# Two tokens to a one-hot row set, and four tokens' rows streamed per product, in a parallel attention and expert-lookup kernel

## The chip, the cores and the metric

The kernel runs on one core of a Trainium2 chip. The metric is the device time of one execution in microseconds. Engines are named as the profile names them: PE (TensorE, with its weight loads as PEld), DVE (VectorE), ACT (ScalarE), POOL (GpSimd), SP (SyncE).

## The reference

The input `x` has 2048 tokens of 512 elements. It is normalised, and two branches are added to it: attention with 32 heads of 16 elements that share one key and one value head, and a product-key expert layer, which alone matters here.

```python
    q = jnp.einsum("nd,dhc->nhc", xf, w_q)          # 32 heads
    s1 = jnp.einsum("nhd,ed->nhe", q[..., :dk], k1)  # 64 scores per head
    s2 = jnp.einsum("nhd,ed->nhe", q[..., dk:], k2)
    # the two best of each, the two best sums of the four pairs: top_s, top_e
    g = _softmax(top_s, axis=-1)
    act = _gelu(jnp.einsum("nd,nhkd->nhk", xf, u[top_e]))
    out = jnp.einsum("nhk,nhk,nhkd->nd", g, act, v[top_e])
```

Each token so picks 64 (head, choice) slots out of 4096 experts, each with a gate.

## The kernel before, in words

Tokens are tiled by 128; four tiles make a group of 512. For the groups 0 and 1 the kernel gathers the picked rows of `u` and `v` by indirect DMA and sums them on DVE. For the groups 2 and 3 it works densely (`dense`, L656): it forms the whole gate matrix, tokens by 4096 experts, on TensorE, then computes all 4096 activations of each token (`pact`, L733), weights them with the gate matrix and multiplies with all of `v` (`pout`, L861).

The gate matrix is formed from one-hot rows. An expert number is split into a part `a` of 128 values and a part `b` of 32 values (`batch`, L563, computes both as `df1` and `df2`, L634 to L638). The 64 slots of a token lie on partitions. A gate is kept as two halves, the F16 value of the gate times 8192 and the rest (L647 to L649), so that F16 products lose nothing; the two halves lie on partitions 0 to 63 and 64 to 127 of the same token, and both index rows are stored twice for it. `spread` (L755) transposes the three arrays to slots by tokens on TensorE (`ptd`) and copies them to F16 (`tr`).

Then, for each 16 tokens (`TB`), `onehot` (L779) lets DVE compare a table `io` with the indices: `oa` is 128 rows by 128 values of `a` by 16 tokens (L783), `ob` 128 rows by 32 values of `b` by 16 tokens (L785), which is multiplied by the gates (L786). For each token one product, `oa` of the token as weights (128 by 128) and `ob` of the token as moving data (128 by 32), gives its 128 by 32 gate matrix in PSUM (`pg`, L815). Sixteen of these fill one PSUM tile of 512 columns. ACT copies it in two pieces to a staging tile, sorted by `b` (`copies`, L818 to L820), and after every 64 tokens SP stores it to DRAM (L825, L827). A group has 32 rounds of this (`NQ`), and `onehot` runs two rounds ahead.

The order of the work is written out by hand. PE, DVE, ACT, POOL and SP keep the order in which the program issues instructions. The outer loop (`att_steps`, L1138) makes one turn per attention step: scores `sc` (4 products of 64 rows, in pairs on the two row halves), `pv` (16 products) for the step before, scores again, then `fill` (L1315), which takes the next pieces of the expert layer from a generator (`score_thread`). Each piece yields a cost, and `fill` stops when the costs reach the smaller of a line that rises to `FILL` over the steps and the spent cost plus `MOST`. A round of one-hot products yields 2.0 (L848). While they run (`dense_on` is 2) the step's gathered sums are put behind the fill. Copies and similar work are queued in `POST` and come before the next piece or in the middle of the next step. PSUM tiles of tag `x` (`pg`, `ptd`, `pact`, `psc`, `pout`) share three buffers.

Of the kernel before, what the change touches and what calls it, by code (L numbers as in the profile page):

```python
# [11 lines left out]
F32 = mybir.dt.float32  # L12
F16 = mybir.dt.float16
# [10 lines left out]
P = 128  # L24
# [6 lines left out]
GT = 4  # L31
# [10 lines left out]
NWK = 8  # L42
NIDX = 9
GS = 8192.0
FILL = 948.0
SCALE = DH ** -0.5
LIMIT2 = 25000.0
C_IN = 0.7978845608028654
# [1 line left out]
HOLD = 44  # L50
MOST = 4.0
UNIT = 0.235


@with_exitstack
def tile_kernel(ctx, tc, x, wq, wkv, wo, wqT, kT, uv, ub, vb, out):
# [498 lines left out]
    DT, gated_all = [], []  # L555

    def dense_tiles():
        for _ in range(2):
            da = big.tile([P, 2, D], F32, name="da", tag="da", bufs=2)
            for i in range(2):  # L560
                DT.append(da[:, i, :].rearrange("p (t r s) -> p t r s", t=GT, r=2))

    def batch(ph, c, b):  # L563
        m8, i8 = M8.pop((ph, c, b)), I8.pop((ph, c, b))
        sh = [P, BT, 4]
        T = lambda name, dt=F32, s=sh, bufs=1: small.tile(s, dt, name=name, bufs=bufs)
# [24 lines left out]
        fv = fi.rearrange("p t (h s) k -> p t h s k", s=2)  # L591
        i1a, i1b, i2a, i2b = fv[:, :, :, 0, 0], fv[:, :, :, 0, 1], fv[:, :, :, 1, 0], fv[:, :, :, 1, 1]
        e1, e2 = T("e1"), T("e2")
        stt = V.scalar_tensor_tensor
        den = T("den")
        if ph < NSP:
            idx = T("idx", I32, [P, BT, 4, 2], NIDX)
            i1 = fv[:, :, :, 0, :]
            G_.tensor_scalar(i1, i1, float(E), None, op0=OP.mult)
            G_.tensor_add(e1, i1a, i2b)  # L600
            G_.tensor_add(e2, i1b, i2a)
            G_.tensor_add(i1a, i1a, i2a)
# [21 lines left out]
        df1, df2, dgt = DT[:3]  # L624
# [12 lines left out]
        for r in range(2):  # L637
            G_.tensor_add(df1[:, :, r, w], hi, ii[:, 0])  # L638

        def gates():  # L640
            V.tensor_scalar(den, ex, 2.0, 2.0, op0=OP.mult, op1=OP.add)
            gg = T("gd", F32, [P, BT, 8])
            gv = gg.rearrange("p t (h k) -> p t h k", k=2)
            V.reciprocal(gv[:, :, :, 0], den)
            V.tensor_mul(gv[:, :, :, 1], ex, gv[:, :, :, 0])
            gh = T("gh", F16, [P, BT, 8])
            V.tensor_scalar(gh, gg, GS, None, op0=OP.mult)  # L647
            V.tensor_copy(dgt[:, :, 0, w], gh)
            stt(dgt[:, :, 1, w], gg, GS, gh, op0=OP.mult, op1=OP.subtract)  # L649
            if c == NC - 1:  # L650
                gated_all.append(True)

        exp_later(gates)


    def dense(DG, after):  # L656
# [67 lines left out]
        early = []  # L724
        on_act(lambda: early.extend(half_split(b, 0) for b in range(2)))
        yield 0.0
        df1, df2, dgt = DT[:3]

        def activations(b, us, p):
            n = 0  # L730
# [24 lines left out]
        def spread(n):  # L755
            p = xtile("ptd")
            for j in range(GT):
                nc.tensor.transpose(p[:, j * P:(j + 1) * P], DT[n][:, j].rearrange("p r s -> p (r s)"), ident)
            nc.scalar.copy(tr[:, n, :], p)

        io = kt(F16, (P, P, TB))
        nc.sync.dma_start(io, d_io)
        tr = kt(F16, (P, 3, 512))
        hh = late[0].tile([P, 2, 512], F32, name="gy", tag="gy", bufs=3)
        yield from first(0)
        rest_of_first = first(1)
# [3 lines left out]
            yield 0.45  # L770
        while not gated_all:
            yield None
        spread(2)
        yield 0.45
# [4 lines left out]
        def onehot(q):  # L779
            if q < NQ:  # L780
                tb = q * TB
                oa = kt(F16, (P, P, TB))
                nc.vector.tensor_tensor(out=oa, in0=io, in1=bc(0, tb, P), op=OP.is_equal)  # L783
                ob = obs[:, q % 3]
                nc.vector.tensor_tensor(out=ob, in0=io[:, :NB, :], in1=bc(1, tb, NB), op=OP.is_equal)  # L785
                nc.vector.tensor_mul(ob, ob, bc(2, tb, NB))  # L786
                OH[q] = oa, ob

        def first_gates():
# [10 lines left out]
                    ACC[t] = da[:, i, :]  # L800
                    LIVE.add(t)

        obs = kt(F16, (P, 3, NB, TB))
        onehot(0)
        yield from rest_of_first
        onehot(1)
        for q in range(NQ):
            t0, ql = q // 4 * 64, q % 4
            if ql == 0:
                st = [late[0].tile([P, 16, 64], F32, name="gst", tag="wd", bufs=4) for _ in range(2)]  # L810
            onehot(q + 2)
            oa, ob = OH.pop(q)
            p = xtile("pg")
            for i in range(TB):
                nc.tensor.matmul(p[:, i * NB:(i + 1) * NB], oa[:, :, i], ob[:, :, i], start=True, stop=True)  # L815
            pv_ = p.rearrange("p (t b) -> p b t", b=NB)

            def copies(pv_=pv_, st=st, ql=ql, t0=t0):  # L818
                for hb in range(2):
                    nc.scalar.copy(st[hb][:, :, ql * TB:(ql + 1) * TB], pv_[:, 16 * hb:16 * hb + 16, :])  # L820
                if ql == 3:
# [12 lines left out]
            POST.append((copies, lambda: None))  # L834

            if q in (NQ - 16, NQ - 12):
                later_split((NQ - 16, NQ - 12).index(q))
            if q == NQ - 3:
                on_act(lambda: halves.__setitem__(2, half_split(2, 0)))
            if q == NQ - 3:  # L840
                quiet[0] = 3
            if q == NQ - 2:
# [3 lines left out]
            if q == NQ - 1:  # L846
# [521 lines left out]
```

## Time and profile before

| | |
|---|---|
| median of 3 runs | 1927.19 us |
| lowest, highest run | 1919.88, 1936.14 us |
| the profiled execution | 1931.19 us |
| its span, first to last instruction | 1929.5 us |
| mean granted TensorE clock | 0.98 |
| PE busy | 1865.4 us |
| DVE busy | 1633.0 us |
| ACT busy | 1294.3 us |
| one-hot products `pg` (L815), first and last start | 613.0 and 1528.2 us |

Times in views are microseconds from the start of the span. The one-hot stage comes twice, once for each dense group, at about 609 to 717 us and 1418 to 1528 us. In rows of busy time by window, each engine's busy time in the window is followed by its number of instructions, then come the mean granted clock of TensorE in that window (1.00 is full speed), the share of DMA time and the DMA rate. In rows of groups stand the line, the engine, the operation, the tiles, the shape and the count; then busy time, mean nanoseconds of one instruction, and idle time before it with what ended it. Successive instructions overlap, so the distance of two starts is shorter than an instruction. In the chain of waits, a row is start, duration, engine, tile, line and count.

### The profile page before, as it was taken

The numbers are of one execution on the slowest core, as the hardware profiler recorded it, in microseconds if no ns is written. First come the engines' busy times: TensorE is split into PE (matmuls) and PEld (weight loads), VectorE is DVE, ScalarE is ACT, GpSimd is POOL, SyncE is SP. The second block draws the span as 40 slices with busy tenths as digits, with TensorE's granted clock in tenths as the row PEclk, the third lists the DMA queues.
The fourth block names the chain that finished last, engine by engine and source line by source line (L and its number), as shares of the span: only waits on it lengthen the run. The fifth ranks groups of instructions, "written<-read, shape, count | busy, mean of one in ns | idle before, by whom it ended". The sixth has DMA issues, their size and how long they took to land.

```text
span 1929.5 us, 35007 instructions
## 1 busy us (share of the span) xinstructions
PE 1865.4 (97%) x10990; PEld 995.2 (52%) x10990; DVE 1633.0 (85%) x6381; ACT 1294.3 (67%) x1803; POOL 693.5 (36%) x920
## 2 busy tenths in 40 slices
PE   6879999999999999999999999999999999999998
PEld 4544444555555544555555454555555555555553
DVE  6626788889998976999999897899988879999994
ACT  3336666655557887877877555555578877888873
POOL 1202334334453213343444354344522124344430
PEclk9989999999999989999999999999999999999999
DMA  7856878887673668799889977877645778899882
GB/s 269 300 202 229 291 263 294 287 294 277 231 268 121 216 213 260 248 283 292 267 288 308 353 278 241 295 243 264 216 138 194 267 222 291 271 284 284 283 274 83
DMA packets 245724, 491.14 MB, mean 255 GB/s; under 512 B 93972, under 2 KB 106260, under 8 KB 245532
## 3 DMA queue, kind: packets, MB, share of 16 engines
q0 software_dynamic: 73728, 268.47, 41.4%
q1 hardware_dynamic: 170568, 219.56, 34.9%
q8 instruction: 88, 1.44, 0.3%
q10 hardware_dynamic: 1236, 0.82, 0.1%
q14 instruction: 104, 0.85, 0.1%
HBM read 427.41 MB, written 56.07 MB: 251 GB/s over the span
## 4 chain that ended last, share of the span: by engine, by line
PE 84%; DVE 3%; ACT 2%; issue 1%; DMA 1%; another core or an unknown queue 0%; SPq 0%; ACTq 0%; DVEq 0%
PE pv L341 23%; PE psc L531 18%; PE sc L327 17%; PE pact L733 10%; PE pout L861 9%; PE pg L815 2%; PE pwo L434 2%; ACT pt L330 2%; PE pw L487 2%; DVE oh L783 1%; DMA wk<-dw 1%; DVE xa L1023 1%; DMA wqt<-in_wqT_dram 0%; PE pwt L494 0%; PE pwl L409 0%
## 5 line engine op out<-in xcount | busy, mean ns | idle before, releaser
L330 ACT ACTIVATE pt<-sc 128x1024 f32<-128x1024 f32 x1024 | 994.4, 1026 | 459.2 <-PE sc L327 405.9
L976 POOL DMA_INDIRECT g<-in_uv_dram,idx x512 | 555.0, 1084 | 1009.5 <-DVE xa L1023 531.9
L341 PE MATMUL pv<-pt,vaug 128*32 128x512 f32 x4096 | 508.9, 615 | 0.0
L531 PE MATMUL psc<-wk,xt 128*128 128x512 f32 x1536 | 390.9, 402 | 6.6 <-DVE wk L497 3.5
L327 PE MATMUL sc<-qa,kaug 64*128 64x512 f32 x2048 | 387.0, 453 | 7.7 <-ACT pt L330 6.9
L1023 DVE SCALAR_TENSOR_TENSOR xa<-g,w,xa 128x512 f32<-128x512 f32 x512 | 371.5, 744 | 0.1
L988 DVE CUSTOM_DVE_ANT_0 g<-g,xa 128x512 f32<-128x512 f32 x512 | 335.2, 680 | 6.6 <-DMA g<-in_uv_dram,idx 6.6
L531 PEld LDWEIGHTS psc<-wk,xt 128*128 128x128 f32 x1536 | 279.4, 189 | 110.5 <-issue 40.3
L327 PEld LDWEIGHTS sc<-qa,kaug 64*128 64x128 f32 x2048 | 157.1, 187 | 326.1 <-ACT pt L330 194.3
L341 PEld LDWEIGHTS pv<-pt,vaug 128*32 128x32 f32 x4096 | 108.8, 111 | 255.7 <-issue 254.1
L546 DVE FIND_INDEX8 i<-m,psc 128x8 uint32<-128x64 f32 x1024 | 206.2, 220 | 0.0
L733 PE MATMUL pact<-xt,wk 128*128 128x512 f32 x768 | 196.0, 400 | 0.0
L861 PE MATMUL pout<-wk,wd 128*128 128x512 f32 x768 | 194.9, 402 | 0.2 <-DVE wd L919 0.2
L544 DVE MAX8 m<-psc 128x8 f32<-128x64 f32 x1024 | 146.1, 213 | 41.2 <-PE psc L531 40.0
L861 PEld LDWEIGHTS pout<-wk,wd 128*128 128x128 f32 x768 | 140.8, 188 | 47.4 <-issue 5.5
L733 PEld LDWEIGHTS pact<-xt,wk 128*128 128x128 f32 x768 | 139.4, 188 | 48.6 <-issue 17.9
L864 DVE TENSOR_TENSOR da<-da,pout 128x512 f32<-128x512 f32 x128 | 82.7, 678 | 10.1 <-PE pout L861 8.6
L698 DVE TENSOR_TENSOR wk<-rw,wk 128x512 fp32r<-128x512 f32 x128 | 84.7, 682 | 7.1 <-ACT wk L697 7.1
L783 DVE TENSOR_TENSOR oh<-oh 128x2048 f16<-128x2048 f16 x64 | 78.0, 1219 | 2.3 <-PE pg L815 1.7
L815 PEld LDWEIGHTS <-oh 128*128 128x128 f16 x1024 | 68.4, 163 | 13.6 <-issue 4.8
L815 PE MATMUL pg<-oh 128*128 128x32 f16 x1024 | 73.7, 246 | 0.8 <-DVE oh L786 0.7
L697 ACT CAST wk<-rw 128x512 fp32r<-128x512 f32 x128 | 74.0, 632 | 0.0
(159 smaller groups left out, 1356.4 us busy)
## 6 DMA issues: line engine op xcount, KB each, us to landing
wk<-dw SPq DMA_DIRECT2D x96, 512.0 KB
wqt<-in_wqT_dram SPq DMA_DIRECT2D x32, 512.0 KB
dw<-wk SPq DMA_DIRECT2D x32, 512.0 KB
rw<-in_ub_dram SPq DMA_DIRECT2D x64, 256.0 KB
rw<-in_vb_dram SPq DMA_DIRECT2D x64, 256.0 KB
gy<-dg SPq DMA_DIRECT2D x64, 256.0 KB
qa<-dqh SPq DMA_DIRECT2D x128, 64.0 KB
g<-in_uv_dram,idx POOLq DMA_INDIRECT x512
```

Of the source, the lines that this page charges most:

```text
L327: nc.tensor.matmul(p[:, b, :], kaug[o:o + 64, kc * P:(kc + 1) * P], QA[u][o:o + 64, i, :], start=True, stop=True)
L330: nc.scalar.activation(pt, p, AF.Exp, scale=SCALE)
L341: nc.tensor.matmul(PV[u][32 * j:32 * j + 32, :], vaug[:, kc, :], pt[:, b, :], start=kc == 0, stop=kc == 15)
L531: nc.tensor.matmul(p, XT[k][:, a, j * P:(j + 1) * P], WC[n_][k][:, bb, :], start=n == 0, stop=n == 11)
L544: nc.vector.max(m8[:, jb, s, :], p[:, s * E:(s + 1) * E])
L546: nc.vector.max_index(i8[:, jb, s, :], m8[:, jb, s, :], p[:, s * E:(s + 1) * E])
L733: nc.tensor.matmul(p, us[:, a, k * P:(k + 1) * P], XT[k][:, c, :], start=n == 0, stop=n == 11)
L815: nc.tensor.matmul(p[:, i * NB:(i + 1) * NB], oa[:, :, i], ob[:, :, i], start=True, stop=True)
L861: nc.tensor.matmul(p, wd[0][:, a, j * P:(j + 1) * P], vs[:, c, :], start=n == 0, stop=n == 5)
L976: nc.gpsimd.indirect_dma_start(out=gt, out_offset=None, in_=uv, in_offset=bass.IndirectOffsetOnAxis(ap=IDX[ph, c, ti][:, s:s + 1], axis=0))
L988: nc.vector.tensor_tensor_reduce(u, u, XN[TPH * ph + ti], scale=1.0, scalar=0.0, op0=OP.mult, op1=OP.add, accum_out=a[:, i:i + 1])
L1023: nc.vector.scalar_tensor_tensor(acc, v, w[:, i:i + 1], acc, op0=OP.mult, op1=OP.add)
```

## The change

The rows of a product are shared by two tokens instead of two gate halves: partitions 0 to 63 hold the 64 slots of an even token, partitions 64 to 127 those of the odd token after it. A round covers 16 pairs, 32 tokens, so there are 16 rounds. `oa` and `ob` are compared once per pair; `ob` is then multiplied by the upper and by the lower gate halves into two tiles. The index arrays are stored once, the gate halves as arrays of their own, four arrays in all, and `spread` brings the parity apart with an identity matrix read in steps of two.

For each pair there are four products instead of two: for each gate half `r` one on each row half `h`, with 64 rows. Those of the two gate halves add up in PSUM, and each row half has a PSUM tile of its own. The moving data are `WIDE` = 4 tokens' `ob` rows, 128 columns, though only the first 32 belong to the weights' token; the other 96 are overwritten by the products of the following tokens. `copies` writes every second token. The round's cost, the constants and the points at which later work is queued are fitted to 16 rounds.

```diff
-FILL = 948.0
+FILL = 935.0
+WIDE = 4
...
     def dense_tiles():
-        for _ in range(2):
-            da = big.tile([P, 2, D], F32, name="da", tag="da", bufs=2)
-            for i in range(2):
-                DT.append(da[:, i, :].rearrange("p (t r s) -> p t r s", t=GT, r=2))
+        da = big.tile([P, 4, GT, 64], F32, name="da", tag="da", bufs=2)
+        DT.extend(da[:, i] for i in range(4))
...
-        for r in range(2):
-            G_.tensor_add(df2[:, :, r, w], hi, ii[:, 1])
+        G_.tensor_add(df2[:, :, w], hi, ii[:, 1])
...
-            V.tensor_copy(dgt[:, :, 0, w], gh)
-            stt(dgt[:, :, 1, w], gg, GS, gh, op0=OP.mult, op1=OP.subtract)
+            V.tensor_copy(dgh[:, :, w], gh)
+            stt(dgl[:, :, w], gg, GS, gh, op0=OP.mult, op1=OP.subtract)
...
-        NQ = 512 // TB
+        NQ = 512 // (2 * TB)
...
             for j in range(GT):
-                nc.tensor.transpose(p[:, j * P:(j + 1) * P], DT[n][:, j].rearrange("p r s -> p (r s)"), ident)
-            nc.scalar.copy(tr[:, n, :], p)
+                for h in range(2):
+                    nc.tensor.matmul(p[64 * h:64 * h + 64, 64 * j:64 * j + 64], DT[n][:, j, :], ident[:, h::2],
+                                     start=True, stop=True)
+            nc.scalar.copy(tr[:, n, :], p[:, :256])
...
-                ob = obs[:, q % 3]
-                nc.vector.tensor_tensor(out=ob, in0=io[:, :NB, :], in1=bc(1, tb, NB), op=OP.is_equal)
-                nc.vector.tensor_mul(ob, ob, bc(2, tb, NB))
+                ob = obs[:, q % 2]
+                nc.vector.tensor_tensor(out=ob[:, 1], in0=io[:, :NB, :], in1=bc(1, tb, NB), op=OP.is_equal)
+                for i in range(2):
+                    nc.vector.tensor_mul(ob[:, i], ob[:, 1], bc(2 + i, tb, NB))
...
-            onehot(q + 2)
+            onehot(q + 1)
             oa, ob = OH.pop(q)
-            p = xtile("pg")
+            ps_ = [xtile("pg") for _ in range(2)]
             for i in range(TB):
-                nc.tensor.matmul(p[:, i * NB:(i + 1) * NB], oa[:, :, i], ob[:, :, i], start=True, stop=True)
+                for r in range(2):
+                    for h in range(2):
+                        o = slice(64 * h, 64 * h + 64)
+                        n = min(WIDE, TB - i)
+                        nc.tensor.matmul(ps_[h][:, i * NB:(i + n) * NB], oa[o, :, i],
+                                         ob[o, r, :, i:i + n].rearrange("p b t -> p t b"),
+                                         start=r == 0, stop=r == 1)
...
-            yield 2.0
+            yield 3.6
```

More of the change, by code (lines that the diff above doesn't have):

```diff
@@ L623, in batch @@
             dense_tiles()
-        df1, df2, dgt = DT[:3]
+        df1, df2, dgh, dgl = DT
         ii = T("ii", F32, [P, 2, BT, 8])
@@ L633, in batch @@
         G_.tensor_scalar(hi, ii[:, 1], 32.0, -32.0, op0=OP.is_ge, op1=OP.mult)
-        for r in range(2):
-            G_.tensor_add(df2[:, :, r, w], hi, ii[:, 1])
+        G_.tensor_add(df2[:, :, w], hi, ii[:, 1])
         G_.tensor_scalar(hi, hi, -2.0, None, op0=OP.mult)
-        for r in range(2):
-            G_.tensor_add(df1[:, :, r, w], hi, ii[:, 0])
+        G_.tensor_add(df1[:, :, w], hi, ii[:, 0])
         def gates():
@@ L726, in dense @@
         yield 0.0
-        df1, df2, dgt = DT[:3]
         def activations(b, us, p):
@@ L757, in spread @@
             for j in range(GT):
-                nc.tensor.transpose(p[:, j * P:(j + 1) * P], DT[n][:, j].rearrange("p r s -> p (r s)"), ident)
-            nc.scalar.copy(tr[:, n, :], p)
+                for h in range(2):
+                    nc.tensor.matmul(p[64 * h:64 * h + 64, 64 * j:64 * j + 64], DT[n][:, j, :], ident[:, h::2],
+                                     start=True, stop=True)
+            nc.scalar.copy(tr[:, n, :], p[:, :256])
         io = kt(F16, (P, P, TB))
         nc.sync.dma_start(io, d_io)
-        tr = kt(F16, (P, 3, 512))
+        tr = kt(F16, (P, 4, 256))
         hh = late[0].tile([P, 2, 512], F32, name="gy", tag="gy", bufs=3)
@@ L772, in dense @@
             yield None
-        spread(2)
-        yield 0.45
+        for n in (2, 3):
+            spread(n)
+            yield 0.45
         dense_on[0] = 2
@@ L801, in load_totals, with copies @@
                     LIVE.add(t)
-        obs = kt(F16, (P, 3, NB, TB))
+        obs = kt(F16, (P, 2, 2, NB, TB))
         onehot(0)
         yield from rest_of_first
-        onehot(1)
         for q in range(NQ):
-            t0, ql = q // 4 * 64, q % 4
+            t0, ql = q // 2 * 64, q % 2
             if ql == 0:
                 st = [late[0].tile([P, 16, 64], F32, name="gst", tag="wd", bufs=4) for _ in range(2)]
-            onehot(q + 2)
+            onehot(q + 1)
             oa, ob = OH.pop(q)
-            p = xtile("pg")
+            ps_ = [xtile("pg") for _ in range(2)]
             for i in range(TB):
[L815 to L821, printed above, removed]
+                for r in range(2):
[5 more added lines that the diff above has]
+                                         start=r == 0, stop=r == 1)
+            def copies(ps_=ps_, st=st, ql=ql, t0=t0):
+                for h in range(2):
+                    pb = ps_[h].rearrange("p (t b) -> p b t", b=NB)
+                    for hb in range(2):
+                        to = st[hb][:, :, ql * 2 * TB:(ql + 1) * 2 * TB].rearrange("p b (t h) -> p b t h", h=2)
+                        nc.scalar.copy(to[:, :, :, h], pb[:, 16 * hb:16 * hb + 16, :])
+                if ql == 1:
                     def part(b0, b1, st=st, t0=t0):
@@ L834, in dense @@
             POST.append((copies, lambda: None))
-            if q in (NQ - 16, NQ - 12):
-                later_split((NQ - 16, NQ - 12).index(q))
-            if q == NQ - 3:
+            if q in (NQ - 8, NQ - 6):
+                later_split((NQ - 8, NQ - 6).index(q))
+            if q == NQ - 2:
                 on_act(lambda: halves.__setitem__(2, half_split(2, 0)))
-            if q == NQ - 3:
+            if q == NQ - 2:
                 quiet[0] = 3
-            if q == NQ - 2:
+            if q == NQ - 1:
                 dense_on[0] = 3
@@ L845, in dense @@
                 later_split(2)
-            if q == NQ - 1:
                 later_split(3)
-            yield 2.0
+            yield 3.6
         held, ready, used = [], [], [0]
```

## The prediction

> **What bounds the kernel now.** I read the page first, then the one-hot stage in the windows of busy time, then the chain of waits, then single groups.
>
> ```profile
> PE 1865.4 (97%) x10990; PEld 995.2 (52%) x10990; DVE 1633.0 (85%) x6381; ACT 1294.3 (67%) x1803; POOL 693.5 (36%) x920
> PEclk9989999999999989999999999999999999999999
> ```
>
> TensorE is busy 97% of the span, so its work sets the time. The digits of the granted clock hide what matters here; the windows show it. The stage with the one-hot products comes twice; the first two rows are its two passes (17 attention steps each), then two undisturbed steps with 32 products, one with 16, and every step with a lowered clock. A step is one turn of the attention loop: sc, pv, sc, then whatever fills it. The third number is busy PE; PEclk stands third from the end.
>
> ```profile
> core 0: us, PE busy (x) PEld busy (x) DVE busy (x) ACT busy (x) POOL busy (x), PEclk, DMA share, GB/s
> 609.47:710.30 100.83, 99.82 (x905) 52.23 (x904) 94.42 (x193) 85.45 (x142) 21.48 (x18) 0.90 0.63 204
> 1426.52:1528.33 101.81, 97.76 (x907) 52.30 (x905) 94.23 (x189) 86.33 (x143) 23.23 (x20) 0.92 0.63 210
> 615.21:620.56 5.35, 5.35 (x60) 3.10 (x58) 5.21 (x14) 4.92 (x9) 0.00 (x0) 1.00 0.08 21
> 1511.37:1516.72 5.35, 5.35 (x58) 3.10 (x57) 5.28 (x11) 5.00 (x10) 0.00 (x0) 1.00 0.98 317
> 705.59:710.30 4.71, 4.53 (x42) 2.18 (x40) 4.43 (x12) 4.71 (x10) 1.15 (x1) 1.00 0.98 349
> 636.93:642.88 5.95, 5.95 (x42) 2.27 (x40) 5.81 (x17) 3.88 (x8) 0.00 (x0) 0.71 0.98 302
> 654.20:661.29 7.09, 7.09 (x58) 3.51 (x56) 6.99 (x13) 5.60 (x12) 0.12 (x1) 0.76 0.51 199
> 677.45:684.54 7.09, 7.09 (x58) 3.50 (x57) 7.02 (x12) 5.25 (x9) 3.35 (x3) 0.76 0.55 187
> 684.54:691.60 7.06, 7.06 (x60) 3.35 (x58) 6.38 (x14) 5.20 (x10) 1.15 (x1) 0.76 0.84 263
> 691.60:698.63 7.03, 7.03 (x59) 3.34 (x57) 5.28 (x12) 5.08 (x10) 0.00 (x0) 0.76 0.46 171
> 698.63:705.59 6.96, 6.96 (x59) 3.30 (x57) 5.88 (x12) 4.82 (x8) 3.34 (x3) 0.75 0.39 109
> 1431.80:1439.44 7.64, 7.22 (x56) 3.45 (x57) 7.57 (x14) 6.10 (x10) 2.11 (x2) 0.78 0.47 128
> 1439.44:1446.43 6.99, 6.99 (x60) 3.44 (x58) 6.85 (x17) 5.00 (x9) 0.00 (x0) 0.76 0.70 236
> 1457.25:1464.29 7.04, 5.75 (x59) 3.23 (x58) 6.94 (x16) 4.85 (x9) 2.75 (x3) 0.94 0.99 308
> 1464.29:1471.32 7.03, 7.03 (x42) 2.68 (x40) 5.96 (x13) 4.21 (x8) 0.00 (x0) 0.57 0.57 209
> 1494.11:1500.09 5.98, 5.98 (x42) 2.48 (x40) 5.84 (x15) 4.58 (x9) 0.00 (x1) 0.71 0.73 239
> 1528.33:1535.34 7.01, 7.01 (x35) 3.00 (x34) 4.90 (x16) 6.39 (x12) 0.91 (x1) 0.76 0.52 150
> ```
>
> An undisturbed step with 32 products takes 5.35 us and one with 16 takes 4.71. Those with 42 instructions on PE hold 16 products, the others of the stage 32. The eleven rows with a lowered clock exceed their clean length by 1.24 (5.95 against 4.71) to 2.32 us (7.03 against 4.71). The one at 1457.25 is mostly a wait (PE busy 5.75 of 7.04); the other ten exceed by 17.2 us together. The clock explains it: 0.76 over 7.09 us is 3.4 us at half rate, which costs 1.7 us, and 7.09 less 5.35 is 1.74. The chain of waits shows a clean step (first four rows) and a step with the low clock:
>
> ```profile
> 615.28 0.66 PE sc L327 x4
> 615.94 1.85 PE pv L341 x16
> 617.79 0.66 PE sc L327 x4
> 618.46 2.17 PE pg L815 x32
> ...
> 678.18 3.37 PE pv L341 x16
> 681.55 0.79 PE sc L327 x4
> 682.34 2.27 PE pg L815 x32
> ```
>
> It is TensorE all the way round. The low clock falls on pv (3.37 for 1.85) and hardly on the one-hot products (2.27 for 2.17). So the products seem to bring the clock down and the attention pays.
>
> **The change part by part.** First the products. They go from 1024 of 128 rows and 32 columns to 2048 of 64 rows and 128 columns, in row pairs; the instruction order of the changed kernel shows 32 bursts of 64, one burst to a step, where 36 bursts of 16 or 32 stood. So 32 tokens still cost 32 turns of the array, if the two halves run side by side.
>
> ```profile
> L531 PE MATMUL psc<-wk,xt 128*128 128x512 f32 x1536 | 390.9, 402 | 6.6 <-DVE wk L497 3.5
> L327 PEld LDWEIGHTS sc<-qa,kaug 64*128 64x128 f32 x2048 | 157.1, 187 | 326.1 <-ACT pt L330 194.3
> L815 PE MATMUL pg<-oh 128*128 128x32 f16 x1024 | 73.7, 246 | 0.8 <-DVE oh L786 0.7
> 618.39 2.23 PE L815 MATMUL pg<-oh 128*128 128x32 f16 x32
> 617.72 0.30 PEld L327 LDWEIGHTS sc<-qa,kaug 64*128 64x128 f32 x4 [0.84 <-ACT pt L330]
> 25.94 0.44 PE L218 MATMUL pv_t<-ident,kv 32*128 32x32 f32 x4 [0.20 <-ACT kv L203]
> 591.35 3.69 PE L531 MATMUL psc<-wk,xt 128*128 128x512 f32 x15
> 605.76 1.04 PE L758 MATMUL ptd<-ident,da 128*128 128x128 f32 x8
> ```
>
> Today's turn is (2.23 - 0.246) / 31 = 64 ns for 32 columns. A 512-column product turns over in (3.69 - 0.40) / 14 = 235 ns, 0.46 ns per column, so 32 columns are 15 ns of streaming: three quarters of the 64 ns is a floor, not data. 128 columns at 0.46 are 59 ns and fit under it. That the halves run together is what sc does already: its 64-row products come in such pairs, and 4 take 0.66 us, 0.33 per pair of 512 columns, where two in series would be 0.47. Bounds for a pair: 59 ns below (streaming alone), 128 above (two floors in series). Between them lie 83 (a quarter of sc's 0.33) and 107 (the 128-column F32 transpose ptd, (1.04 - 0.29) / 7 with a latency between pg's 0.246 and psc's 0.40). I take 64: the same floor, since the stream fits, and pg is the nearest row. A burst then keeps its length. A pair dearer by 1 ns costs 1.0 us over 1024 pairs.
>
> Second the clock. Streaming fills 15 of 64 ns today and 59 of 64 after it, about as dense as the psc products, and through the stretch of those between the passes the page's clock digits are 9. I take the 17.2 us as gone, and 1.6 us of the step at 1528.33, which has the low clock just behind the stage.
>
> Third the sum for the stage. The two passes take 202.64 us and hold 62 of the 64 groups of 16 tokens; the other two lie in mixed steps, 16 x 64 ns and a switch of 0.2, 2.4 together. They hold 34 attention steps; after it 32 hold all groups, and two go to steps elsewhere at 0.66 + 1.85 + 0.66 = 3.17 each. So like for like it is 202.6 + 2.4 - 6.3 = 198.7 us today. Clean steps would be 28 x 5.35 + 6 x 4.71 = 178.1; 24.5 are excess, 17.2 of it clock and 7.3 other waits, 0.21 per step, which I keep. A burst of today also has an edge: 2.17 us from its first product to the next sc is 31 turns and 0.19, where a turn is 0.064; the array goes over from 128-row to 64-row work there, and the other way at the start. The new products are 64-row work as sc is, so up to 0.12 at each end can go. I count one end, as ScalarE stands near: its busy time in the clean steps is 4.92 and 5.00, and its work per 32 tokens stays. So 32 x (5.35 + 0.21 - 0.12) = 174.1, a gain of 24.6. Bounds of the step: 5.0 below (ScalarE), 5.9 above (rival E).
>
> Fourth the work off the chain.
>
> ```profile
> L783 DVE TENSOR_TENSOR oh<-oh 128x2048 f16<-128x2048 f16 x64 | 78.0, 1219 | 2.3 <-PE pg L815 1.7 <-issue 0.4 <-ACT oh L759 0.2
> L785 DVE TENSOR_TENSOR oh<-oh 128x512 f16<-128x512 f16 x64 | 26.7, 417 | 0.0
> L786 DVE TENSOR_TENSOR oh<-oh 128x512 f16<-128x512 f16 x64 | 27.2, 425 | 2.3
> L820 ACT COPY gst<-pg 128x256 f32<-128x256 f32 x128 | 42.8, 405 | 0.2 <-PE pg L815 0.2
> ```
>
> VectorE makes 32 wide comparisons instead of 64, 32 narrow ones instead of 64, and the same 64 gate products: (1219 + 417) x 32 = 52 us less. I count nothing for it: the chain runs over TensorE, the 94.4 busy us of VectorE in a pass of 100.8 at most gave some of the small waits, which I kept. The copies stay 128 of 256 elements; writing every second word could cost or save a little, and the next step's exponentials cover it. GpSimd loses two additions per batch and is 36% busy. SP's stores of the gates keep their number and size. The spreading of indices takes 64 small products and 8 copies where 24 and 6 stood: 64 x 64 ns less 24 x 107 is 1.5 us, and I count 2. The pacing constants (3.6 per 32 tokens for 4.0, the target lower by 13) move work between steps, not in amount.
>
> Sum: -24.6 - 1.6 + 2.0 = -24.2. The profiled execution took 1931.19 us (span 1929.5), so 1907; the median of the runs shown is 4.0 lower, 1927.19, and gives 1903. I say 1904.
>
> **The rivals.** B, strided reading (ends slower). The 128 columns lie 32 bytes apart, and no row streams such columns for longer than the floor. If each costs 0.86 ns, as a column of sc's weights does ((0.30 - 0.187) us from the first pair's load to the second's, 128 columns), a pair takes 110 ns and adds 1024 x 46 ns = 47 us: 1951. It decides from 64 + 23 = 87 ns per pair on. At the far end, were all of today's 64 ns reading, it would be 256 ns, +197 us, 2101. Against the far end: L218's 32 columns lie side by side and take the same ((0.44 - 0.222) / 3 = 73 ns with the first start). The Trainium skill, SBUF — State Buffer, section Specifications (TRN2), states that each access that crosses to a new 16-byte line pays a penalty, which would make every one of these columns pay; it gives no figure, and no row here shows it.
>
> C, halves in series: 128 ns per pair, +65 us, 1969. sc's pairs speak against it.
>
> D, the clock still falls: then 17.2 + 1.6 us stay, 1923. For it: the chip's rule isn't in the trace, and PE reads busy through all of the stage. The Trainium skill, TensorE: Matmul & The Clock Gate, Part 1, ties the half rate to an idle window of about 3.4 us; by that rule a TensorE that reads busy 99% should not drop, and wider products would mend nothing. The 0.76 steps with PE busy 7.09 of 7.09 disagree with it, unless short streams count as idle.
>
> E, a new wait: a burst now fills two of three PSUM tiles at once, and both are emptied only in the next step, behind two exponentials, where the first tile of a pair was emptied within the burst's own step. With 0.46 us per step for it (about one copy, 0.405), steps take 5.9: +15, 1919.
>
> **How the numbers follow.** Forecast 0.50, B 0.20, C 0.11, D 0.09, E 0.10. The forecast's own range is 1893 (steps of 5.1, by ScalarE's bound) to 1916. The range 1893 to 1952 takes in E, D and most of B, and leaves out C and B's far end. About 1% can be told from no change, 1908 to 1946. Faster: 0.76 of the forecast, 0.38. Same: the rest of it 0.12, E, D, 0.02 of B, 0.33. Slower: B and C, 0.29.
>
> **What would show it.** 2048 products; bursts of 64 in 2.1 to 2.3 us; PEclk 1.00 through both passes and pv at 1.85; steps of 5.3 to 5.6; L783's group at 39 us. Bursts of 3.5 us with a full clock mean B, 4.1 mean C; 0.76 in the windows means D; sc waiting on exponentials, or products on copies, with a clean clock means E.

## The result and the profile after

The changed kernel takes 2135.44 us (median of 4 runs, 2131.53 to 2137.17) beside 1931.66 of the kernel before (4 runs): ratio 1.1065, 95% interval 1.1033 to 1.1097. It is slower by a tenth, where 1904 was forecast. The profiled execution has a span of 2135.4 us, 205.9 more than the 1929.5 of before. The page of the kernel after, its first line, the granted clock, and the groups of the products and of attention:

```profile
PE 2060.9 (97%) x12118; PEld 1096.8 (51%) x12118; DVE 1588.7 (74%) x6317; ACT 1297.3 (61%) x1805; POOL 679.9 (32%) x888
PEclk9989999999997769999999999999977689999999
L818 PE MATMUL pg<-oh 64*128 64x128 f16 (+3 forms) x2048 | 231.2, 397 | 0.6 <-ACT gst L827 0.3
L342 PE MATMUL pv<-pt,vaug 128*32 128x512 f32 x4096 | 538.9, 646 | 0.0
L328 PE MATMUL sc<-qa,kaug 64*128 64x512 f32 x2048 | 402.4, 469 | 10.8 <-ACT pt L331 7.1
```

TensorE is still the bound, 97% busy, with 195.5 us more to do. The one-hot products went from 73.7 to 231.2 us of busy time. The two dips of the clock, to 7 and 6 in tenths, are the two one-hot passes. Attention, which the change doesn't touch, pays for them: pv took 508.9 and takes 538.9, sc took 387.0 and takes 402.4. The windows of the two passes (16 steps each) and of two steps, with the columns of the prediction's first windows:

```profile
616.66:808.99 192.33, 191.85 (x1410) 101.75 (x1410) 71.38 (x160) 83.92 (x139) 21.04 (x18) 0.71 0.33 106
1530.34:1730.68 200.34, 197.66 (x1504) 106.20 (x1505) 75.90 (x173) 89.75 (x149) 22.99 (x21) 0.73 0.32 103
638.76:651.38 12.62, 12.62 (x94) 6.38 (x92) 4.16 (x11) 4.99 (x8) 0.00 (x0) 0.64 0.71 236
651.38:662.87 11.49, 11.49 (x95) 6.31 (x92) 1.89 (x5) 5.03 (x8) 0.00 (x0) 0.80 0.01 1
```

The two steps shown take 12.62 and 11.49 us, and nearly all the others 11.4 to 12.7, where 5.44 was forecast. A clock of 0.71 over 192.33 us is 192.33 x 0.29 / 0.5 = 112 us at half rate, where the first pass of before, 0.90 over 100.83 us, had 20. PE is busy all through (191.85 of 192.33), and DVE and ACT are busy for 71 and 84 us of it, so no other engine holds it up. The chain of waits over a step and a half (start, duration, engine, tile, line, count):

```profile
651.58 1.01 PE sc L328 x4
652.59 2.81 PE pv L342 x16
655.40 0.66 PE sc L328 x4
656.07 7.02 PE pg L818 x59
663.09 1.01 PE sc L328 x4
664.10 3.57 PE pv L342 x16
```

The burst of 64 products takes 7.02 us; a burst for the same 32 tokens took 2.17. Over 32 bursts that is 32 x 4.85 = 155 us. The scores behind a burst take 1.01 for 0.66 and pv 2.81 to 3.57 for 1.85; by the two groups above that is 30.0 + 15.4 = 45.4 us. The two together, 200.6, are nearly all of the 205.9. What one turn costs is seen in a narrow window of the timeline of PE, three pairs of four tokens:

```profile
644.67 0.90 PE L818 MATMUL pg<-oh 64*128 64x128 f16 x6
```

The six products run from the first start to the last end in 0.90 us; less one product of 0.417 (the median of the line) that is two turns of 0.24 us. The medians over all pairs, from the starts in the trace's records, are 240 ns for four tokens, 181 to 184 for three, 122 to 126 for two and 65 for one. So a turn of four tokens costs 1.87 ns per column, and it takes the same 240 ns at full and at half clock. In 28 of the 32 bursts the two halves of a pair start 0 to 42 ns apart, 10 in the median; in the other four one half runs most of a turn ahead of the other. The work off the chain is as it was counted (minimum, median and maximum in ns, then first and last start):

```profile
L782 DVE TENSOR_TENSOR oh<-oh x32: 1214/1220/1227, 614.0 to 1697.7; 128x2048 f16<-128x2048 f16 x32
L784 DVE TENSOR_TENSOR oh<-oh x32: 417/422/427, 615.1 to 1706.5; 128x512 f16<-128x512 f16 x32
L786 DVE TENSOR_TENSOR oh<-oh x64: 424/425/428, 615.6 to 1707.5; 128x512 f16<-128x512 f16 x64
L827 ACT COPY gst<-pg x128: 381/422/456, 629.8 to 1734.2; 128x256 f32<-128x256 f32 x128
```

### The profile page after: what moved, and what is told of

Same layout as the page of the kernel before. It is cut to its first block, busy times and chain, and to the rows that moved or that the text cites. A ratio compares the mean times of both kernels' runs of the same rounds, so it can differ in the third digit from the quotient of the medians.

```text
span 2135.4 us, 37163 instructions
## 1 busy us (share of the span) xinstructions
PE 2060.9 (97%) x12118; PEld 1096.8 (51%) x12118; DVE 1588.7 (74%) x6317; ACT 1297.3 (61%) x1805; POOL 679.9 (32%) x888
## 4 chain that ended last, share of the span: by engine, by line
PE 81%; DMA 4%; DVE 4%; ACT 2%; issue 2%; SPq 0%; another core or an unknown queue 0%; ACTq 0%; DVEq 0%
PE pv L342 22%; PE psc L532 16%; PE sc L328 15%; PE pg L818 11%; PE pact L729 7%; PE pout L867 6%; PE pwo L435 2%; ACT pt L331 2%; DMA gy<-dg 1%; PE pw L488 1%; DVE xa L1029 1%; DMA rw<-in_vb_dram 1%; DMA wk<-dw 1%; DVE g L994 1%; DMA dinv<-rc 0%
## 5 line engine op out<-in xcount | busy, mean ns | idle before, releaser
L342 PE MATMUL pv<-pt,vaug 128*32 128x512 f32 x4096 | 538.9, 646 | 0.0
L328 PE MATMUL sc<-qa,kaug 64*128 64x512 f32 x2048 | 402.4, 469 | 10.8 <-ACT pt L331 7.1
L328 PEld LDWEIGHTS sc<-qa,kaug 64*128 64x128 f32 x2048 | 166.9, 197 | 338.1 <-ACT pt L331 165.4
L818 PE MATMUL pg<-oh 64*128 64x128 f16 (+3 forms) x2048 | 231.2, 397 | 0.6 <-ACT gst L827 0.3
L818 PEld LDWEIGHTS <-oh 64*128 64x128 f16 x2048 | 159.0, 145 | 77.5 <-issue 10.0
L1017 DVE SCALAR_TENSOR_TENSOR w<-gth,ga 128x4 f32<-128x4 f32 x128 | 20.6, 161 | 208.2 <-ACT gth L1010 207.8
```

What stands on the lines that cost most here:

```text
L328: nc.tensor.matmul(p[:, b, :], kaug[o:o + 64, kc * P:(kc + 1) * P], QA[u][o:o + 64, i, :], start=True, stop=True)
L342: nc.tensor.matmul(PV[u][32 * j:32 * j + 32, :], vaug[:, kc, :], pt[:, b, :], start=kc == 0, stop=kc == 15)
L818: nc.tensor.matmul(ps_[h][:, i * NB:(i + n) * NB], oa[o, :, i], ob[o, r, :, i:i + n].rearrange("p b t -> p t b"), start=r == 0, stop=r == 1)
```

## The experiments

The first theory, S, was that the 32-byte step of the columns costs about 1.8 ns each. Its rivals were H, that products on 64-row halves are slow, and C, that the clock is the main cause. After the first four kernels S was narrowed to L: each 16-byte line that the moving rows open costs about 1.9 ns. Beside it K was put for the clock: it is kept up by the columns that stream per nanosecond. Each kernel is compared with the kernel before on the same chip.

**One token to a product (w1).**

```diff
-WIDE = 4
+WIDE = 1
```

> The changed kernel with WIDE = 1: each of the 2048 64-row products streams the 32 columns of its own token only. Theory S (stride): a streamed column that lies 32 bytes from the one before it costs about 1.8 ns of TensorE, whatever the clock, so 128 columns took 240 ns per pair and 32 take about 62; a burst of 64 products then lasts 2.0 to 2.2 us instead of 7.3, and the kernel comes to 1890 to 1935 us. Theory H (halves): the pairs of 64-row F16 products are slow in themselves (two halves, or two sums into PSUM); then a pair stays above 120 ns, a burst above 3.9 us, and the kernel above 1985 us. Theory C (clock): the time went mainly to the half-rate clock; then the burst hardly shortens and the low stretches stay, over 2050 us. By S the low clock stays in part, as 32 columns of 62 ns are as thin as before.

Measured: 1930.21 us (10 runs), ratio 1.0031, interval 1.0011 to 1.0051. The page's group of w1, then its timeline from the scores ahead of a burst to those behind it:

```profile
L818 PE MATMUL pg<-oh 64*128 64x32 f16 x2048 | 75.4, 246 | 2.8 <-ACT gst L827 2.8
645.63 0.73 PE L328 MATMUL sc<-qa,kaug 64*128 64x512 f32 x4
646.21 2.35 PE L818 MATMUL pg<-oh 64*128 64x32 f16 x64
648.32 0.76 PE L328 MATMUL sc<-qa,kaug 64*128 64x512 f32 x4
```

A turn is (2.35 - 0.246) / 31 = 68 ns. The whole loss goes with the three additional tokens, and 0.3% is left, so the pairing and the 64-row halves cost little: H falls. DVE has as much less to do as in the changed kernel, and the time doesn't show it. At the edges of the burst something is won: from scores to burst 0.58 us for 0.66, from burst to scores 2.11 for 2.17. The windows of w1's two passes:

```profile
615.76:703.62 87.86, 85.70 (x1410) 51.25 (x1410) 69.40 (x157) 81.94 (x139) 21.97 (x18) 1.00 0.71 229
1418.78:1523.61 104.83, 99.41 (x1503) 56.56 (x1502) 73.96 (x170) 88.02 (x149) 23.47 (x21) 0.93 0.59 196
```

The clock is 1.00 in the first pass and 0.93 in the second, where the kernel before had 0.90 and 0.92, although w1 streams as few columns per nanosecond as that kernel. A short thin burst, then, lowers the clock at some times and not at others.

**The widening without the pairing (before_wide).** The kernel before, with products of 128 rows that stream four tokens:

```diff
-                nc.tensor.matmul(p[:, i * NB:(i + 1) * NB], oa[:, :, i], ob[:, :, i], start=True, stop=True)
+                n = min(WIDE, TB - i)
+                nc.tensor.matmul(p[:, i * NB:(i + n) * NB], oa[:, :, i],
+                                 ob[:, :, i:i + n].rearrange("p b t -> p t b"), start=True, stop=True)
```

> The kernel before with the widening alone: 1024 products of 128 rows, each streaming the strided columns of four tokens (128) instead of one (32). Theory S: a product turns over in 240 ns instead of 64, 32 of them take 7.5 us instead of 2.1, and with the clock lower for longer the kernel comes to 2110 to 2160 us: the whole loss without any pairing. Theory H: 64 to 70 ns, 1905 to 1935 us.

Measured: 2109.76 us, one run. The group and a burst:

```profile
L817 PE MATMUL pg<-oh 128*128 128x128 f16 (+3 forms) x1024 | 230.2, 401 | 0.1
655.87 7.20 PE L817 MATMUL pg<-oh 128*128 128x128 f16 x32
```

The burst is as long as that of the changed kernel, with 32 products for its 64. The widening alone makes nearly the whole loss.

**The same columns side by side (contig).** The changed kernel with the narrow rows stored token by token, so that the 128 columns of a product are contiguous:

```diff
-        obs = kt(F16, (P, 2, 2, NB, TB))
+        obs = kt(F16, (P, 2, 2, TB, NB))
...
-                                         ob[o, r, :, i:i + n].rearrange("p b t -> p t b"),
+                                         ob[o, r, i:i + n, :].rearrange("p t b -> p (t b)"),
```

> The changed kernel with WIDE = 4, but the narrow one-hot rows stored token by token, so that the 128 streamed columns are one run of 256 bytes; VectorE writes them in steps of 64 bytes for it. Theory S: pairs at 55 to 70 ns, bursts of 1.8 to 2.2 us, clock 1.00 in the stage, 1890 to 1920 us if VectorE's steps cost nothing, up to 1940 if its narrow groups double (3 x 32 x 0.42 us is 40 us). Theory H: pairs at 240 ns, about 2135 us.

Measured: 2071.87 us (4 runs), ratio 1.0755, interval 1.0719 to 1.0791. Its products are cheap and its DVE is not; the groups of the page:

```profile
L819 PE MATMUL pg<-oh 64*128 64x128 f16 (+3 forms) x2048 | 100.8, 271 | 117.7 <-DVE oh L787 113.3
L787 DVE TENSOR_TENSOR oh<-oh 128x512 f16<-128x512 f16 x64 | 154.4, 2413 | 2.5
L785 DVE TENSOR_TENSOR oh<-oh 128x512 f16<-128x512 f16 x32 | 78.0, 2439 | 0.0
```

A turn with 128 contiguous columns takes about 63 ns at full clock (the median of the records), 107 at half clock. So the forecast's sentence that 128 columns fit under the floor holds for contiguous columns. But the writes of DVE now lie 64 bytes apart, and an instruction takes 2.4 us where 0.42 stood; PE waits 113.3 us for it. The kernel shows the price of a turn; its time, far above the 1890 to 1940 that were expected, is DVE's and says nothing on the turn.

**Runs inside a line (runs, runs8).** A run here is a stretch of adjacent values. The layout of the changed kernel, with the columns streamed value by value: the four tokens of a value lie side by side, 8 bytes, then comes the next value. In runs8 the window of tokens also ends at every eighth token, so that no run crosses a 16-byte line; this is the diff of runs8, and runs keeps `min(WIDE, TB - i)`:

```diff
-                        n = min(WIDE, TB - i)
-                        nc.tensor.matmul(ps_[h][:, i * NB:(i + n) * NB], oa[o, :, i],
-                                         ob[o, r, :, i:i + n].rearrange("p b t -> p t b"),
+                        n = min(WIDE, 8 - i % 8)
+                        nc.tensor.matmul(ps_[h].rearrange("p (b t) -> p b t", t=TB)[:, :, i:i + n], oa[o, :, i],
+                                         ob[o, r, :, i:i + n],
```

> The changed kernel with WIDE = 4, but the same 128 columns streamed in the order in which they lie: for each value of b the four tokens side by side (runs of 4 F16 elements, 8 bytes), written to PSUM in that order too. Theory S by place in memory: only a jump of 32 bytes costs, 32 jumps as with one token, so a pair takes 60 to 70 ns, a burst 2.0 to 2.2 us; the array then streams nearly all the time, the granted clock stays at 1.00 in the stage, and the kernel comes to 1890 to 1920 us. Theory S by element (any column not read as one long run costs 1.8 ns): pair 240 ns, about 2135 us. Theory H: the pair stays at 240 ns, about 2135 us.

> The run that streams tokens side by side, with windows that end at a 16-byte border (up to four tokens, fewer for the last three of each eight). In that run the windows that started at tokens 5, 6 and 7 of eight took about 118 ns per pair and the others 62 to 75. Theory L (line): TensorE pays about 1.9 ns for each 16-byte line that it opens, 32 lines without a crossing and 64 with one; then every pair takes 60 to 75 ns, the products take 35 to 38 us per pass instead of 42.8, and the kernel is 10 to 16 us faster than that run, 1908 to 1920 us here, if the clock stays up. Theory S by element: no change from that run, 1931 us. If the fewer columns let the clock fall, 5 to 10 us are lost again.

Measured: runs 1931.37 us (10 runs), ratio 1.0032, interval 1.0007 to 1.0056; runs8 1921.69 (12 runs), ratio 0.9982, interval 0.9966 to 0.9998. First a burst of runs, then one of runs8, then the window of a pass of runs8:

```profile
649.55 2.80 PE L818 MATMUL pg<-oh 64*128 64x128 f16 x64
```

```profile
649.27 2.46 PE L818 MATMUL pg<-oh 64*128 64x128 f16 x64
618.49:707.50 89.01, 87.06 (x1409) 52.99 (x1410) 69.44 (x157) 82.00 (x139) 21.94 (x18) 1.00 0.71 227
L867 PE MATMUL pout<-wk,wd 128*128 128x512 f32 x768 | 197.9, 405 | 9.1 <-DVE gy L910 5.1
```

The same 128 columns from the same tile cost 62 to 82 ns a turn, if they stay in 32 lines. In runs the windows that start at token 5, 6 or 7 of eight reach into a second line for every value, which makes 64 lines, and those turns take 105 to 130 ns. The clock in the pass is 1.00, where before it was 0.90; as w1 had 1.00 in its first pass too, one pass alone proves little. Both kernels took longer than expected (1890 to 1920 for runs, 1908 to 1920 for runs8). The last row shows what takes part of the gain back: pout waits 9.1 us, where the kernel before waited 0.2; in the changed kernel it is 5.1, in w1 4.2.

**The widening alone, inside a line (before_runs8, before_runs3, before_runs2).** The kernel before, 128 rows to a product, with at most four, three or two tokens:

```diff
+WIDE = 4
...
+                n = min(WIDE, 8 - i % 8)
+                nc.tensor.matmul(p.rearrange("p (b t) -> p b t", t=TB)[:, :, i:i + n], oa[:, :, i],
+                                 ob[:, :, i:i + n], start=True, stop=True)
```

> The kernel before with the widening alone, in its harmless form: 128-row products, up to four tokens side by side within a 16-byte line, PSUM in that order. Theory L: a product keeps its 64 to 70 ns. Theory K (clock by streamed columns): up to 128 columns in 66 ns keep the granted clock at 1.00 in the stage, the 17 to 19 us that the low stretches cost come back, and the kernel takes 1900 to 1912 us against 1921. If the clock falls for another reason than thin streams (waits, the switch of the array between row sizes), the low stretches stay and the time is 1915 to 1930. If the pairing itself were what keeps the clock up, the same.

> The same with three tokens (96 columns). Theory K: clock 1.00 in both one-hot stages, products 62 to 72 ns, time 1908 to 1915, beside the 1914 of four tokens. If the time lies above 1917, the gain of four tokens was not the clock's alone.

> The kernel before with products that stream two tokens (32 columns, in two runs of adjacent tokens, so that no run crosses a 16-byte line) instead of four or one. Theory L (each 16-byte line of the moving rows that is opened costs about 1.9 ns): a product keeps the 62 to 76 ns of its neighbours with four and with one. Theory K (the clock is kept by the number of columns that a turn streams): with half the columns of the four-token kernel the clock in the one-hot stages stays at 1.00 if 64 columns are enough, and the time is 1905 to 1914, at or below the 1914 of four tokens since the products are shorter; if 64 are too few, half-clock stretches of several us come back and the time is 1915 to 1922. A rival, that the clock fell in the kernel before by chance of the run and not by the columns, gives 1920 to 1928 with stretches like its 20 us.

Measured: four tokens 1913.82 us (12 runs), ratio 0.9942, interval 0.9925 to 0.9959; three tokens 1911.94 (6 runs), 0.9943, 0.9922 to 0.9963; two tokens 1914.84 (12 runs), 0.996, 0.9942 to 0.9977. All three are faster than both kernels, by a small amount (0.4 to 0.6% against the kernel before) that is clear of the noise; four tokens came out 2 us above the range that was expected. The window of a pass and three groups of the kernel with four tokens, then the window of a pass with two:

```profile
605.39:705.40 100.01, 98.19 (x952) 56.43 (x952) 97.19 (x202) 92.27 (x153) 21.44 (x18) 1.00 0.67 216
L342 PE MATMUL pv<-pt,vaug 128*32 128x512 f32 x4096 | 493.6, 598 | 0.0
L328 PE MATMUL sc<-qa,kaug 64*128 64x512 f32 x2048 | 380.9, 448 | 7.0 <-ACT pt L331 6.8
L817 PE MATMUL pg<-oh 128*128 128x128 f16 (+3 forms) x1024 | 78.9, 243 | 2.8 <-DVE oh L787 2.8
```

```profile
606.70:706.52 99.82, 96.25 (x952) 54.31 (x951) 97.09 (x201) 91.82 (x153) 21.48 (x18) 1.00 0.68 216
```

The clock is 1.00 in the pass with four tokens and with two (64 columns). Over all executions of these kernels the mean clock of the whole span has a median of 0.99, in the kernel before 0.98. Attention, which the edit doesn't touch, gets back 15.3 us in pv and 6.1 in sc against the profiled execution of before, one of its longer ones; the products take 5.2 more. By the medians the gain is 11 us. It comes without the pairing, and where the clock is back, so it is the clock's. Which of the three is best is not told apart: their intervals overlap.

**The line as the unit (g4, g4_wide).** The changed kernel with narrow rows in groups of four tokens, so that the columns of one token lie 8 bytes apart, two to a line. g4 streams one token to a product, g4_wide four, three, two and one, as the groups end. The diff is that of g4_wide; in both, DVE's writes are reordered to match:

```diff
-        obs = kt(F16, (P, 2, 2, NB, TB))
+        obs = kt(F16, (P, 2, 2, TB // 4, NB, 4))
...
-                        n = min(WIDE, TB - i)
+                        n = 4 - i % 4
...
-                                         ob[o, r, :, i:i + n].rearrange("p b t -> p t b"),
+                                         ob[o, r, i // 4, :, i % 4:].rearrange("p b t -> p t b"),
```

> The changed kernel with one token per product (32 columns) and the narrow rows stored in groups of four tokens, so that neighbouring columns lie 8 bytes apart, two to a 16-byte line. Theory L: 16 lines cost 30 ns, so a pair is bounded by what else there is, the weight load; if that is shorter than 62 ns, pairs fall to 40 to 55 ns and the products to 25 to 30 us per pass; if the load is the floor of 60, pairs stay at 60 to 66. VectorE writes runs of 8 bytes now: where writing every 64 bytes made its narrow operations 2400 ns instead of 420, runs of four could take 600 (little change in the time) to 2400 (about 2070 us).

> The changed kernel with its second rows stored in groups of four tokens, so that a product's columns lie 8 bytes apart, two to each 16-byte line, instead of 32 bytes apart; products stream four, three, two and one tokens, as the groups end. Theory L: 128 columns open 64 lines, about 120 ns per pair, 96 columns about 90, 64 and 32 columns about 62; some 85 ns on average, a few half-clock us, 1925 to 1960. If the cost is by the column that isn't adjacent to the last, whatever the step: 240, 180, 120 and 62 ns, and a time between 2040 and 2140. If only steps over some width cost: 62 to 66 ns throughout and 1918 to 1930.

Measured: g4 1928.58 us (10 runs), ratio 1.0024, interval 1.0007 to 1.004; g4_wide 1936.6, one run. A burst of g4, then one of g4_wide and the window of its pass:

```profile
642.28 2.18 PE L819 MATMUL pg<-oh 64*128 64x32 f16 x64
```

```profile
650.64 2.82 PE L820 MATMUL pg<-oh 64*128 64x128 f16 x64
618.38:712.17 93.79, 92.82 (x1409) 58.79 (x1410) 69.86 (x159) 82.55 (x139) 21.97 (x18) 1.00 0.67 216
```

With half the lines to open, one token's turn stays at 63 ns, so this is a floor in which the reading of the moving rows has no part; but a product of g4 is shorter, 210 ns in the median for 246. What sets the floor was not tried. Every product also loads 128 columns of weights, and these lie 32 bytes apart in all of these kernels. In g4_wide the turns are 120, 93, 64 and 50 ns for 64, 48, 32 and 16 lines; the 50, behind three longer turns, is below the floor, so the floor isn't a fixed cost of a product. The two longer ones fit L: 64 x 1.87 = 120, 48 x 1.87 = 90. The reading by the single column (240) and that of a free 8-byte step (63) both fall. All turns side by side, medians at full clock, good to some 3 ns:

| columns and how they lie | lines opened | ns per turn |
|---|---|---|
| 128, 32 bytes apart (the change, before_wide) | 128 | 240 |
| 96, 32 bytes apart | 96 | 181 to 184 |
| 128, 8 bytes apart (g4_wide) | 64 | 120 |
| 64, 32 bytes apart | 64 | 122 to 126 |
| 128, in runs of four (runs8) | 32 | 76 |
| 32, 32 bytes apart (w1) | 32 | 66 |
| 32, 8 bytes apart (g4) | 16 | 63 |
| 128, contiguous (contig) | 16 | 63 |

L doesn't account for the whole row of runs8: 32 x 1.87 is 60, and it takes 76. Its products also write PSUM in runs of four; whether the rest lies there was not tried.

**What brings the clock down (w1_x3, runs8_x3).** w1 and runs8 with every pair of products issued three times over, which makes bursts of 6 to 7 us like those of the change, once thin and once dense:

```diff
-                for r in range(2):
+                for r in (0, 1) * 3:
```

> The changed kernel with one token to a product (32 columns, 32 bytes apart) and every pair of products issued three times over, the same result each time: bursts of about 6.3 us at half a column per nanosecond, as long and as thin as those of the changed kernel, but without a wide product. The two repeats add 2048 turns of 65 ns, 133 us, to the 1930 of one token to a product. Theory K (the clock goes where few columns per nanosecond stream for long): half-clock stretches of some 100 us in each pass as in the changed kernel, pv and sc pay 20 to 25 us per pass, time 2095 to 2115. A rival, that the wide strided products are needed to bring the clock down: stretches of 0 to 20 us and 2060 to 2075.

> The changed kernel with its columns streamed token by token inside a 16-byte line, and every pair of products issued three times over: bursts of about 7 us as well, at 1.1 to 1.7 columns per nanosecond. The repeats add 2048 turns of 75 ns, 154 us, to 1922. Theory K: the clock stays at 1.00 in both passes, time 2070 to 2085. A rival, that any long burst of 64-row F16 products brings the clock down whatever it streams: half-clock stretches of some 100 us per pass and 2110 to 2130.

Measured, one run each: w1_x3 2138.27 us, runs8_x3 2088.17, beside 1932.08 of the kernel before. For w1_x3 and then for runs8_x3, the clock of the page, the products, and the window of the first pass:

```profile
PEclk9989999999987679999999999999967789999999
L818 PE MATMUL pg<-oh 64*128 64x32 f16 x6144 | 218.7, 247 | 9.1 <-issue 7.5
614.03:804.00 189.97, 184.37 (x3458) 127.36 (x3458) 71.38 (x160) 83.92 (x139) 21.05 (x18) 0.72 0.34 109
```

```profile
PEclk9999999999999999999999999999999999999999
L818 PE MATMUL pg<-oh 64*128 64x128 f16 (+1 forms) x6144 | 227.0, 240 | 8.3 <-issue 6.3
616.16:782.90 166.74, 161.96 (x3458) 126.22 (x3458) 71.30 (x160) 83.11 (x139) 21.30 (x18) 0.99 0.39 124
```

Equally many products, PE busy to the same 97% of the pass, and a clock of 0.72 against 0.99. The thin bursts cost as much of the clock as the change does, without a wide product; the dense ones nearly nothing. K holds for long bursts, and the rival that the wide strided products are needed falls. Both times are above what was expected, runs8_x3 by 3 us, w1_x3 by 23: in the first pass the repeats took 76 us from start to start instead of 66, and attention paid 26 a pass instead of 20 to 25.

For short bursts the kept traces tell more. The granted clock changes in pieces of 3.41 us. Over the 14 traces there are 244 pieces at half rate that follow one at full rate. Ahead of 240 of them fewer than 4050 columns (1.2 per ns, attention's included, a product of 64 rows counted as half) had started in 3.41 us, up to 0.6 us before the piece. Of 7365 pieces that stayed at full rate 147 came behind so few. In the passes, 16 of 51 such stretches fall below that count in the kernel before, 12 of 50 in w1, 33 of 50 in the changed kernel and 5 of 97 in runs8_x3. The count and the 0.6 us are fitted to these traces; this is a reading of traces, and no kernel was run to try it.

## Why the prediction was wrong, point by point

**The step that failed** is the cost of a product: "three quarters of the 64 ns is a floor, not data. 128 columns at 0.46 are 59 ns and fit under it." The 0.46 ns is the price of contiguous columns. These lie 32 bytes apart and cost 1.87 ns each, so the term of 64 ns for a pair measured 240, 155 us over the 32 bursts. The floor exists (63 ns with 16 lines to open, contig and g4), but 32 lines x 1.87 = 60 ns is the same length, so two limits stood in the one measured 64 ns, and the row couldn't tell which of them held. The forecast took the one that the change doesn't lengthen.

**Rival B** was right in kind and undersized. Its price of 0.86 ns per column (its own row gives (0.30 - 0.187) / 128 = 0.88, 3 us more) gave 1951. Its far end, "were all of today's 64 ns reading", gave 256 ns a pair and 2101, near the 240 ns that came. It was set aside because the 32 contiguous columns of L218 take about the same, 73 ns. That argument fails: those columns show a floor, and the reading has its own 60 ns beside it. A row that takes as long for another reason doesn't exclude the costlier reason. The Trainium skill, SBUF — State Buffer, section Specifications (TRN2), had named the penalty for each new 16-byte line; the runs agree, and put 1.87 ns on it. It also says that full bandwidth needs at least two hits to a line; here two are not enough, for at two to a line 128 columns take 120 ns beside 63 contiguous.

**The clock** was placed rightly and sized wrongly. Right: the products bring it down and attention pays, and 17.2 + 1.6 us were to be won. In before_runs8, where the passes are at 1.00, pv and sc are 21.4 us shorter. Wrong: "about as dense as the psc products". The streams did not get denser: 128 columns in 240 ns are 0.53 per ns, 32 in 64 were 0.50. They only got three times as long, and 20 us of half rate in a pass became 112. **Rival D**, that the clock still falls, so came true, further than it was priced. Its weighing of the Trainium skill (TensorE: Matmul & The Clock Gate, Part 1: half rate after an idle window) is settled by the last two kernels, as far as idle means what the profile shows as idle: at the same busy share of PE the thin stream lost the clock and the dense one kept it, so a PE that reads busy is not enough.

**Rival C** is refuted: in 28 of the 32 bursts the halves start within 42 ns of each other, a pair with one token takes 66 ns, and in before_wide a product without halves takes the same 240. **Rival E** was right in kind: in w1 and runs8 some bursts wait for a copy behind their first pair, 2.8 and 1.9 us in all, not 15. In the change it is 0.6 of waiting in all, hidden behind the long bursts.

**Off the chain.** DVE's one-hot work fell by the 52 us that were counted at nothing, and w1 shows nothing for it. The copies to every second word take 422 ns for 405. The spreading was counted at 2 us; from the first start to the last its products take 1.0 more in the first pass and 0.5 in the second. The switch between 128-row and 64-row work was to bring 0.12 per burst; w1 shows 0.08 ahead of it and 0.06 behind.

**The sum without the reading.** runs8 is the change as the forecast imagined it: dense, with a full clock. It gains 0.2%, not 1.3%. Its turns of four tokens cost 76 ns instead of 64, and pout waits 9.1 us. So the forecast promised too much even for the mechanism that it described. What makes pout wait in every kernel with the pairing (4.2 us and more, 0.2 in the five without) was not tried and stays open; those kernels also carry the pairing's pacing constants. Where the clock's limit lies was not tried either: the bursts that were run stream 0.5 columns per ns or 0.9 and more (before_runs2: 60 on average in 64 ns); the count in the traces puts it near 1.2 over 3.41 us, attention's columns included.

## What to carry to other kernels

Before widening a strided operand, work out how many 16-byte lines the moving rows open per product: here each costs 1.87 ns once that exceeds the floor of some 63, as much as four contiguous columns, and the order in which the columns stream can divide the number by four without moving any data. When a short instruction takes as long as a known floor, that doesn't show that the floor is what holds it; look for a row in which the suspected other cost is larger. A long burst with few columns per nanosecond takes the clock from the work behind it, so part of its price is read in the rows of its neighbours.

## What was new of the hardware

- Moving rows of TensorE cost 1.87 ns per 16-byte line opened (F16, 128 or 64 rows alike), and a turn of 128 such columns takes 240 ns at full and at half clock. Contiguous columns do follow the clock: 63 and 107 ns.
- In a row of equal products, a turn with new weights stays at about 63 ns even where its 32 columns open only 16 lines (g4); behind longer turns it was 50 (g4_wide).
- A busy PE can lose the clock: 0.72 at 0.5 columns per ns in bursts of 6.5 us, 0.99 at some 1.4 per ns (104 columns in 73 ns on average), both 97% busy. In bursts of 2.1 us at 0.5 per ns it was 1.00 in one pass and 0.93 in the other (w1).
- DVE's F16 instruction of 128 by 512 elements takes 0.42 us when it writes adjacent elements, and 2.4 us when it writes one element every 64 bytes. With runs of four (g4) it takes 0.42 again.
